# Half-height matmuls on pairs of tiles for the second dense product, and a new order of all steps

## The chip, the cores and the metric

The kernel runs on one core of a Trainium2 chip. The metric is the device time of one execution in microseconds (us). TensorE (PE) does the matmuls, VectorE (DVE) and ScalarE (ACT) read their results out of PSUM, GpSimd (POOL) helps with SBUF data, and SyncE (SP) issues nearly all transfers. Each engine works through its own instructions in the order in which they were written.

## The reference

`x` is 2048 tokens of 448 values. It is normalised once, and two branches of the result are added to it: an attention whose feature map is a pair of softmaxes (16 heads of 28), and a dense block with the mish activation.

```python
xn = _layernorm(x, axis=-1)
return x + _A_ref(xn, A_wqkv, A_w_phi, A_wo) + _B_ref(xn, B_w1, B_b1, B_w2)
# _A_ref:
pq = jnp.einsum("bhsd,hdf->bhsf", q, w_phi); pk = jnp.einsum("bhsd,hdf->bhsf", k, w_phi)
phi_q = jnp.concatenate([_softmax(pq), _softmax(-pq)], axis=-1)      # phi_k likewise
kv = jnp.einsum("bhsf,bhsd->bhfd", phi_k, v); z = jnp.einsum("bhsf->bhf", phi_k)
num = jnp.einsum("bhqf,bhfd->bhqd", phi_q, kv)
den = jnp.einsum("bhqf,bhf->bhq", phi_q, z)[..., None] + 1e-6
o = num / den                                                        # then o @ wo
# _B_ref:
h = jnp.einsum("bsd,df->bsf", x, w1) + b1                            # F = 1792
act = h * jnp.tanh(softplus(h)); jnp.einsum("bsf,fd->bsd", act, w2)
```

All operands are bf16.

## The kernel before

The 2048 tokens are 16 tiles of 128, taken as 8 pairs `u` (tiles `2u` and `2u+1`). A pair's normalised tokens lie transposed in `xnT`: 448 = 3 x 128 + 64 rows for each tile, arranged so that the halves of 64 rows of both tiles can be worked on side by side. Most products are therefore made of matmuls of 64 rows (half the height of the array), always one on the upper half for one tile and one on the lower half for the other. A step of this kind comes in three passes: A (upper half for the even tile, lower for the odd), B (the halves exchanged) and H (the odd quarter of 64 rows). The two halves of one pass write different PSUM banks; `pe_pass` makes a B pass wait until an A or H pass on the same banks has finished, and the other way round, on PE's own semaphore.

Every piece of work is a named step that records its instructions with what they read and write; waits follow from that. `ORDER` is a list of all step names, written out by hand or by a search, and it alone sets the order on every engine and the choice of PSUM banks (four pairs of banks; `take2` takes the free pair that was used longest ago, and a pair can be held over several steps). The steps:

- `z12` warm-up matmuls on `zeros` (L364), `b1` the bias, `wtk`/`wm` the weight products (L556, L580: `Wpq` and `Wpk`, projections with `w_phi` already in them), `xt` transposes of `xn`
- `v`, `k`, `q`: projections (L423, 64 x 448). ACT takes exponentials of `k` and `q` into `actT` rows and `Eq`; `kn` (DVE, POOL) normalises `k`; `kv` (L649, full 128 rows) sums the products of keys and values over all pairs in one bank, `kvz` adds the epsilon (DVE, L660) and issues the transpose into `KVZ` on SP; `e` transposes `Eq` into `EqT` on SP
- `f0.*`, `f1.*`: first dense product (L423, 64 x 512) for tiles 0 to 7 and 8 to 15, 14 chunks each, with mish on ACT (L699)
- `nd`: scores of one tile, 16 matmuls of 56 rows (L722), followed by six steps of DVE (L738 twice, L742, L744, L746, L748, L749), and `ot`, the transpose of a pair's result on SP
- `wo`: output product of a pair (L845, 64 x 448) in passes A, B, H; `g`: second dense product of one tile, 14 matmuls of 128 rows and 448 columns (L828). Both add into the same bank of the tile, held from the first to the last of the parts; then `finish` (DVE, L793) adds `x`, and `sto` stores. Tile 15 is cut: its last 64 columns come in a piece of their own (L807 to L810).
- `l2s`, `los`: the loads of `W2` and `Wo` on SP's queue

Of the kernel before, what the change touches and what calls it, by code (L numbers as in the profile page):

```python
# [38 lines left out]
class Program:  # L39
# [46 lines left out]
    def dma(self, eng, fn, r=(), w=(), tag=""):  # L86
        return self.op(eng, fn, r, w, dma=True, tag=tag)
# [61 lines left out]
wtk1b wmk0b lqT2 xt3a v2Ha wmk1a v2Ba lqT0 st1 v3Ha lqT1 lqT3 rs1a v3Aa v2Aa st4 rs4p pk v3Ba k3H lx0s k3A qd xn1d  # L149
wmq0d wmq1a k2H k3B lx6s pp k2A st5 q3A xn4d k2B q3B rs5p q2A xt1m l1ts q3H k1A q2H xn5p xt4m st0 v1Ad k1H st6 xt5m e7  # L150
rs0p q2B st7 xn0d v1Bd k1B v1Hd rs7p rs6p k4A k4H q1B k4B xn6d q1H q1A v4Ad k5H xn7d v4Hd k5A v4Bd v5Ad kn1.0 xt0m k5B
v5Bd k0B xt6m v5Hd xt7m v0Ba kn2.1 kn2.0 k0H k0A e3 k6H k6A kn0.0 e2 v6Ba l1ms k6B v0Ha kn0.1 v0Aa v6Aa v6Ha k7H k7A
q4B e6 k7B v7Aa v7Ha kn7.0 q4H q4A q6A q6H v7Ba e9 q6B kn6.0 f0.2B kn5.1 f0.0A f1.2A f0.2A f0.0H f1.2H kn6.1 e5 f1.3B
f0.2H f0.0B e12 f1.2B f1.3A kn4.1 f0.3B kn5.0 f1.3H e13 f0.3H f0.1B e4 f0.3A f0.1H f0.1A q7H q0A kn3.1 q0H kn4.0 q5B
e8 q0B q7B kv5 kn7.1 e0 kv0 kv2 q7A q5A f0.13A q5H f0.13B kv7 kv4 e10 kv6 f0.13H f0.6H f0.6A kn3.0 f0.10A f0.6B kn1.1
f0.10B kv3 kv1 ep f0.10H f1.7H f1.7A e11 f1.9A kvz f1.7B f0.12B f1.5B f0.12A f1.5H f0.5H f1.9H f0.12H l2s f1.9B f1.5A
f0.5A f1.1A nd3 f1.1B f0.5B e15 f1.0A f1.1H f1.13B f1.0H f1.13H f1.0B nd2 los f1.13A ot1m f1.8B f0.9H f1.8A f1.8H nd0
f0.11B f0.9A f0.11A f0.11H f0.7A f0.7H f0.8B nd6 e14 f0.8H f0.9B f0.7B e1 f0.8A f1.12H f1.12A f1.10A nd7 f1.10B f1.4H
f1.10H f1.12B ot3m f1.4A nd1 f1.6B f1.4B f0.4H f1.6A ot0m f0.4A wo1H f1.6H f0.4B nd4 wo1A wo3A wo1B wo3H nd5 ot2m g1
g3 g2 f1.11A f1.11H nd11 wo0B f1.11B wo3B wo0A nd13 wo0H nd10 g6 ot5m g0 g7 g11 nd12 wo2A wo5A sto1 ot6m wo5H wo2B  # L160
nd15 nd9 g10 sto0 g5 nd14 ot7m wo2H wo5B nd8 g4 g9 g14 g13 g12 g8 sto3 ot4m wo4H wo4A wo6B wo7B sto2 wo6H wo6A sto5
wo4B sto4 wo7H wob wo7A g15 stt14 sto6 stt15
"""


# [5 lines left out]
def _kernel(es, nc, A_x, A_wqkv, A_w_phi, A_wo, B_w1, B_b1, B_w2, out):  # L171
    def sb(name, shape, dtype):
        return es.enter_context(nc.sbuf_tensor(name, shape, dtype))
# [76 lines left out]
    def bank(b, n=1):  # L250
        return PS[:, b * TCW:(b + n) * TCW]
# [146 lines left out]
    def pe(fn, r, w, tag, after=()):  # L398
        return op("PE", fn, r=r, w=w, tag=tag, after=after)
# [201 lines left out]
    def xchunk(c, par):  # L601
        return c if c == 3 or par == 0 else 4 + c
# [187 lines left out]
    def finish(t):  # L790
        b = out_bank[t // 2] + t % 2
        n = width(t)
        op("DVE", lambda e: e.tensor_tensor(x_all[:, t, 0:n], bank(b)[:, 0:n], x_all[:, t, 0:n], ALU.add),  # L793
           r=[pb(b), ("x", t)], w=[("out", t)], tag=f"fin{t}")
        if t == LAST:
            last_columns(t, b ^ 1)
        if done[t] == done[t ^ 1] == parts_of(t):
            free2(out_bank[t // 2])
# [33 lines left out]
        if last:  # L832
            finish(t)

    def wo(u, part):
        places = [out_part(2 * u + par) for par in range(2)]
        todo = passes(part)

        def f(e):
            at = {par: [n for n, x in enumerate(todo) if x[1] == par] for par in range(2)}  # L840
            for n, (c, par, (lo, hi)) in enumerate(todo):
                b, first, last = places[par]
                cc = xchunk(c, par)
                w = width(2 * u + par)
                ins = e.matmul(bank(b)[:, 0:w], oT_of(u)[lo:hi, cc * P:(cc + 1) * P], Wo[lo:hi, cc, 0:w],  # L845
                               start=first and n == at[par][0], stop=last and n == at[par][-1])
# [132 lines left out]
```

## Time and profile before

| | |
|---|---|
| runs shown | 151.16, 151.43, 151.85 us, median 151.43 |
| the profiled execution | 150.73 us, span 148.7 us, granted clock 1.000 |
| PE busy | 144.0 us (97%), 1669 matmuls |
| DVE, ACT, POOL busy | 102.7, 74.7 and 38.9 us |
| 64 x 512 matmuls of the first dense product | 392, busy 44.8 us |
| 128-row matmuls of the second (L828) | 224, busy 42.9 us |

A matmul's end in the trace is modelled, and successive matmuls overlap, so busy times of groups on PE count some time twice where pieces alternate. What a piece of work on PE takes is read from one start to the next in the timeline. In a row of the timeline stand the start, the busy time, engine, line, operation, output and inputs, the shape, and how many instructions are merged.

### The profile page before, as it was taken

The numbers are of one execution on the slowest core, as the hardware profiler recorded it, in microseconds if no ns is written. First come the engines' busy times: TensorE is split into PE (matmuls) and PEld (weight loads), VectorE is DVE, ScalarE is ACT, GpSimd is POOL, SyncE is SP. The second block draws the span as 40 slices with busy tenths as digits, with TensorE's granted clock in tenths as the row PEclk, the third lists the DMA queues.
The fourth block names the chain that finished last, engine by engine and source line by source line (L and its number), as shares of the span: only waits on it lengthen the run. The fifth ranks groups of instructions, "written<-read, shape, count | busy, mean of one in ns | idle before, by whom it ended". The sixth has DMA issues, their size and how long they took to land.

```text
span 148.7 us, 3864 instructions
## 1 busy us (share of the span) xinstructions
PE 144.0 (97%) x1669; PEld 74.2 (50%) x1669; DVE 102.7 (69%) x229; ACT 74.7 (50%) x91; POOL 38.9 (26%) x53
## 2 busy tenths in 40 slices
PE   6899999999999999999999999999999999999992
PEld 2365555555444555444444445545555555555561
DVE  0699898996999930407787989529983999930072
ACT  4997999779999999567747661002000000000000
POOL 4424465179999992000000000000000000000000
PEclk9999999999999999999999999999999999999999
DMA  4997997799699069499956053210013130551005
GB/s 131 245 278 216 119 185 149 126 170 344 103 188 196 14 52 132 85 239 295 195 98 125 4 62 62 43 23 0 7 37 86 35 93 0 123 127 58 4 10 175
DMA packets 39964, 17.23 MB, mean 116 GB/s; under 512 B 33932, under 2 KB 39180, under 8 KB 39948
## 3 DMA queue, kind: packets, MB, share of 16 engines
q1 hardware_dynamic: 39776, 16.89, 54.4%
q8 instruction: 13, 0.21, 0.6%
q10 hardware_dynamic: 172, 0.10, 0.2%
q14 instruction: 3, 0.02, 0.0%
HBM read 7.02 MB, written 1.84 MB: 60 GB/s over the span
## 4 chain that ended last, share of the span: by engine, by line
PE 92%; DMA 3%; DVE 2%; SPq 1%; issue 0%
PE PS L423 50%; PE PS L828 29%; PE PS L845 7%; DMA Wkv<-in_A_wqkv_dram 3%; PE PS L722 3%; PE PS L649 2%; PE PS L580 1%; DVE xn L497 1%; SPq L270 1%; PE PS L556 0%; PE PS L505 0%; DVE x_all L793 0%; DVE Eq L512 0%; DVE x_all L814 0%
## 5 line engine op out<-in xcount | busy, mean ns | idle before, releaser
L423 PE MATMUL PS<-xnT,W 64*128 64x512 bf16 x392 | 44.8, 377 | 0.0
L828 PE MATMUL PS<-W,actT 128*128 128x448 bf16 (+1 forms) x224 | 42.9, 351 | 0.0
L699 ACT ACTIVATE actT<-PS,b1T 128x1024 bf16<-128x1024 f32 x28 | 29.8, 1112 | 22.1 <-PE PS L423 22.1
L828 PEld LDWEIGHTS PS<-W,actT 128*128 128x128 bf16 x224 | 21.5, 98 | 19.8 <-issue 0.3
L423 PEld LDWEIGHTS PS<-xnT,W 64*128 64x128 bf16 x392 | 17.9, 94 | 21.9 <-PE PS L423 1.9
L630 POOL TENSOR_TENSOR actT<-actT,rSk 128x896 bf16<-128x896 bf16 x16 | 26.6, 1699 | 5.1 <-DVE rSk L628 5.1
L793 DVE TENSOR_TENSOR x_all<-PS,x_all 128x448 bf16<-128x448 f32 (+1 forms) x16 | 9.2, 613 | 15.2 <-PE PS L845 10.5
L626 DVE TENSOR_REDUCE Sk<-actT 128x32 f32<-128x896 bf16 x16 | 16.6, 1037 | 1.1 <-ACT actT L618 1.1
L618 ACT ACTIVATE actT<-PS 128x896 bf16<-128x896 f32 x16 | 13.7, 920 | 1.8 <-PE PS L423 1.7
L423 PE MATMUL PS<-Wpk,xnT 64*128 64x448 bf16 x112 | 13.2, 349 | 0.0
L423 PE MATMUL PS<-Wkv,xnT 64*128 64x448 bf16 x112 | 12.9, 349 | 0.0
L423 PE MATMUL PS<-Wpq,xnT 64*128 64x448 bf16 x112 | 12.6, 349 | 0.0
L738 DVE COPY Sq<-PS 128x16 f32<-128x16 f32 x32 | 4.0, 167 | 12.0 <-PE PS L722 12.0
L462 DVE BATCH_NORM_STATS2 stats<-x_all 128x6 f32<-128x448 bf16 x14 | 8.4, 601 | 3.4 <-DMA x_all<-in_A_x_dram 3.4
L746 DVE TENSOR_TENSOR v_all<-v_all 128x464 f32<-128x464 f32 x16 | 10.3, 641 | 0.6
L742 DVE TENSOR_TENSOR v_all<-PS,Sq 128x464 f32<-128x464 f32 x16 | 10.3, 641 | 0.5
L749 DVE TENSOR_TENSOR xn<-v_all,rden 128x448 bf16<-128x448 f32 x16 | 10.0, 625 | 0.6
L744 DVE TENSOR_TENSOR v_all<-PS,Sq 128x464 f32<-128x464 f32 x16 | 10.1, 629 | 0.0
L680 ACT ACTIVATE actT<-PS 128x896 bf16<-128x896 f32 x10 | 8.6, 930 | 0.1
L423 PEld LDWEIGHTS PS<-Wpq,xnT 64*128 64x128 bf16 x112 | 5.4, 94 | 5.0 <-ACT actT L680 0.2
L423 PEld LDWEIGHTS PS<-Wkv,xnT 64*128 64x128 bf16 x112 | 5.4, 94 | 5.1 <-ACT actT L618 0.2
L423 PEld LDWEIGHTS PS<-Wpk,xnT 64*128 64x128 bf16 x112 | 5.3, 94 | 5.1 <-issue 0.2
(83 smaller groups left out, 118.8 us busy)
## 6 DMA issues: line engine op xcount, KB each, us to landing
W<-in_B_w_dram SPq DMA_DIRECT2D x1, 1568.0 KB, 7.9
out_dram<-x_all SPq DMA_DIRECT2D x7, 224.0 KB, 2.2
W<-in_B_w_dram SPq DMA_DIRECT2D x1, 1344.0 KB, 7.0
x_all<-in_A_x_dram SPq DMA_DIRECT2D x4, 224.0 KB, 3.1
x_all<-in_A_x_dram SPq DMA_DIRECT2D x2, 448.0 KB, 4.9
Wkv<-in_A_wqkv_dram SPq DMA_DIRECT2D x2, 336.0 KB, 4.8
Wo<-in_A_wo_dram SPq DMA_DIRECT2D x2, 336.0 KB, 6.3
W<-in_B_w_dram SPq DMA_DIRECT2D x2, 224.0 KB, 4.1
```

The source lines that it names most:

```text
L423: ins = e.matmul(o, lhs(c, k), rhs(c, k), start=first and n == at[par][0], stop=last and n == at[par][-1])
L618: op("ACT", lambda e, s=s: e.activation(E_of(u)[:, s, :, :], two(b, D), ACT.Exp, scale=1.0 if s == 0 else -1.0), r=[pb(b), pb(b + 1)], w=[ ...
L626: op("DVE", lambda e: e.tensor_reduce(Sk[u][:, s, :], Eh(), AX.X, ALU.add), r=[("E", u, s)], w=[("Sk", u, s)], tag=f"Sk{u}.{s}")
L630: op("POOL", lambda e: e.tensor_tensor(Eh(), Eh(), ap_on(rSk[u][:, s, 0:1], [[1, 2 * H], [0, DH]]), ALU.mult), r=[("E", u, s), ("rSk", u, ...
L699: op("ACT", lambda e: e.activation(actT[:, fc, q * 1024:(q + 1) * 1024], bank(b, 2), ACT.Mish, bias=b1T[:, fc:fc + 1]), r=[("b1T",), pb(b) ...
L742: op("DVE", lambda e: e.tensor_tensor(tv(t1[i]), num(0), sx(1), ALU.mult), r=[pb(b), pb(b + 1), ("Sq", i, 1)], w=[("t1", i)], tag=f"ta{t}")
L744: op("DVE", lambda e: e.tensor_tensor(tv(t2), num(1), sx(0), ALU.mult), r=[pb(b), pb(b + 1), ("Sq", i, 0)], w=[("t2",)], tag=f"tb{t}")
L746: op("DVE", lambda e: e.tensor_tensor(t1[i], t1[i], t2, ALU.add), r=[("t1", i), ("t2",)], w=[("t1", i)], tag=f"tc{t}")
L749: op("DVE", lambda e: e.tensor_tensor(o_sb[(t // 2) % 2][:, t % 2, :].rearrange("p (h d) -> p h d", d=DH), t1[i][:, :, 0:DH], ap_on(rden[i ...
L793: op("DVE", lambda e: e.tensor_tensor(x_all[:, t, 0:n], bank(b)[:, 0:n], x_all[:, t, 0:n], ALU.add), r=[pb(b), ("x", t)], w=[("out", t)], ...
L828: ins = e.matmul(bank(b)[:, 0:width(t)], actT[:, fc, tok(t)], W2[:, fc, 0:width(t)], start=first and fc == 0, stop=last and fc == FC - 1)
L845: ins = e.matmul(bank(b)[:, 0:w], oT_of(u)[lo:hi, cc * P:(cc + 1) * P], Wo[lo:hi, cc, 0:w], start=first and n == at[par][0], stop=last and ...
```

## The change

Steps `g0` to `g13` are gone. In their place, pairs 0 to 6 get two steps `G{u}A` and `G{u}B`. Each makes, for every one of the 14 chunks of 128 hidden values, one matmul with the upper 64 rows and one with the lower 64: in A the upper half works for the even tile and the lower for the odd, in B they are exchanged. `wo` and `G` share one function, `out_pair`, which gives each pass its place in the accumulation. Tiles 14 and 15 keep `g14` and `g15`. A step that loads `Wk` and `Wv` in one transfer (`lkvs`) is defined and not used by `ORDER`.

`ORDER` is new as a whole. Two lines of it, with the first steps and with the first of the new ones:

```diff
-pv table lx2s lba zero pm st2b lx3s lkms lps st3b lkts z12 pi b1 rs2p pw rs3a xn2d bd lx1s wtk0b lvms lx4s xn3d xt2b
...
+pw pi table lx2s lba zero st2b pm lx3s st3b lkms lps rs2p bd lkts z12 rs3a lx1s lvms xn2d b1 xn3d pv wtk0b xt2b pk
...
+G0A nd11 wo1A G1A nd12 G2A wo0A wo1H nd13 G1B wo1B G0B wo2H nd10 G2B wob ot5m wo2B wo0H wo3A wo0B nd14 G3A wo2A G3B
```

```diff
     def parts_of(t):
-        return 3 if f"wo{t // 2}F" in STEPS else 4
+        return (2 if f"wo{t // 2}F" in STEPS else 3) + (2 if f"G{t // 2}A" in STEPS else 1)
...
-    def wo(u, part):
+    def out_pair(u, part, todo, works, r, tag):
         places = [out_part(2 * u + par) for par in range(2)]
-        todo = passes(part)
 
         def f(e):
             at = {par: [n for n, x in enumerate(todo) if x[1] == par] for par in range(2)}
-            for n, (c, par, (lo, hi)) in enumerate(todo):
+            for n, (c, par, k) in enumerate(todo):
                 b, first, last = places[par]
-                cc = xchunk(c, par)
                 w = width(2 * u + par)
-                ins = e.matmul(bank(b)[:, 0:w], oT_of(u)[lo:hi, cc * P:(cc + 1) * P], Wo[lo:hi, cc, 0:w],
-                               start=first and n == at[par][0], stop=last and n == at[par][-1])
+                lhs, rhs = works(c, par, k, w)
+                ins = e.matmul(bank(b)[:, 0:w], lhs, rhs, start=first and n == at[par][0], stop=last and n == at[par][-1])
             return ins
-        pe_pass(f, [("oT", u)] + [("Wo", n) for n in range(4)], places[0][0], part, f"wo{u}{part}")
+        pe_pass(f, r, places[0][0], part, tag)
...
+    def ffn2_pair(u, part):
+        x = int(part == "B")
+
+        def works(fc, par, k, w):
+            return actT[k[0]:k[1], fc, tok(2 * u + par)], W2[k[0]:k[1], fc, 0:w]
+        out_pair(u, part, [(fc, r ^ x, HALF[r]) for fc in range(FC) for r in range(2)], works,
+                 [("W2",)] + [("act", fc, u // 4) for fc in range(FC)], f"G{u}{part}")
```

PE in the second dense product, before (L828 are the steps `g`, L722 `nd`, L845 `wo`, L423 the end of the first dense product):

```order
L722 MATMUL PS<-KVZ,EqT 128x60 x16
L845 MATMUL PS<-Wo,Wkv 128x448 x20
L722 MATMUL PS<-KVZ,EqT 128x60 x16
L828 MATMUL PS<-W,actT 128x448 x42
L423 MATMUL PS<-xnT,W 128x512 x8
L722 MATMUL PS<-KVZ,EqT 128x60 x16
L845 MATMUL PS<-Wo,Wkv 128x448 x6
L423 MATMUL PS<-xnT,W 128x512 x6
L845 MATMUL PS<-Wo,Wkv 128x448 x12
L722 MATMUL PS<-KVZ,EqT 128x60 x16
L845 MATMUL PS<-Wo,Wkv 128x448 x2
L722 MATMUL PS<-KVZ,EqT 128x60 x16
```

PE at the same place after (L848 is `out_pair`: with `W,actT` a half of `G`, with `Wo` a pass of `wo`; L726 is `nd`):

```order
L427 MATMUL PS<-xnT,W 128x512 x8
L848 MATMUL PS<-W,actT 128x448 x28
L726 MATMUL PS<-KVZ,EqT 128x60 x16
L848 MATMUL PS<-Wo,Wkv 128x448 x6
L848 MATMUL PS<-W,actT 128x448 x28
L726 MATMUL PS<-KVZ,EqT 128x60 x16
L848 MATMUL PS<-W,actT 128x448 x28
L848 MATMUL PS<-Wo,Wkv 128x448 x8
L726 MATMUL PS<-KVZ,EqT 128x60 x16
L848 MATMUL PS<-W,actT 128x448 x28
```

The full-height blocks are gone, a score product stands behind nearly every half of `G`, and three pairs of tiles are open at once; the first `G` comes when the first dense product is done.

PE from the warm-up to the first projections, before (L364 `z12`, L556 and L580 the weight products, L505 `xt`):

```order
L364 MATMUL PS<-zeros 128x512 x12
L693 MATMUL PS<-ident,b_rows 128x14
L556 MATMUL PS<-ident,Wkv 112x128 x8
L505 MATMUL PS<-ident,xn 128x128 x7
L556 MATMUL PS<-ident,Wkv 112x128 x8
L580 MATMUL PS<-Wbd,Eq 128x112 x8
L505 MATMUL PS<-ident,xn 128x128 x7
L423 MATMUL PS<-Wkv,xnT 128x448 x2
L580 MATMUL PS<-Wbd,Eq 128x112 x8
L423 MATMUL PS<-Wkv,xnT 128x448 x26
```

The same after:

```order
L368 MATMUL PS<-zeros 128x512 x12
L697 MATMUL PS<-ident,b_rows 128x14
L560 MATMUL PS<-ident,Wkv 112x128 x8
L509 MATMUL PS<-ident,xn 128x128 x7
L560 MATMUL PS<-ident,Wkv 112x128 x8
L509 MATMUL PS<-ident,xn 128x128 x7
L584 MATMUL PS<-Wbd,Eq 128x112 x16
L427 MATMUL PS<-Wkv,xnT 128x448 x22
```

The second transpose of `xn` went ahead of the weight product, which is now in one piece, and the two matmuls of `v` that stood within it went behind it.

POOL's first instructions of the kernel, before (`zeros` is what the warm-up multiplies):

```order
L339 MEMSET v_all 128x256
L316 MEMSET zeros 128x2
L327 MEMSET mask 112x4
L328 ISA
L328 AFFINE_SELECT mask<-mask 112x4
L331 AFFINE_SELECT mask<-mask 112x4
L319 MEMSET mhalf 128x2
```

and after:

```order
L340 MEMSET Wbd 112x512
L323 MEMSET mhalf 128x2
L324 MEMSET eps_col 128x1
L325 MEMSET ident 128x128
L326 ISA
L326 AFFINE_SELECT ident<-ident 128x128
L320 MEMSET zeros 128x2
```

`zeros` went from second to sixth place of the memory-setting and selecting instructions. Elsewhere: the eight `kv` steps stand on PE in two runs (192 and 64 matmuls) instead of three (96, 96, 64). On SP, `Wo`'s loads went ahead of most transposes of `Eq`, and `W2`'s load from behind the transpose of `KVZ` to behind the first two transposes `ot`. The numbers of instructions on DVE, ACT, POOL and of transfers are the same; PE has 196 matmuls more.

More of the change, by code (lines that the diff above doesn't have):

```diff
@@ L147 @@
 ORDER = """
-pv table lx2s lba zero pm st2b lx3s lkms lps st3b lkts z12 pi b1 rs2p pw rs3a xn2d bd lx1s wtk0b lvms lx4s xn3d xt2b
[L149 to L162, printed above, removed]
+pw pi table lx2s lba zero st2b pm lx3s st3b lkms lps rs2p bd lkts z12 rs3a lx1s lvms xn2d b1 xn3d pv wtk0b xt2b pk
@@ new lines @@
+f0.3A f0.1B f0.3B kn5.1 f0.2A f1.2H f0.2B f0.1H f0.2H f0.0B f1.3B f0.0H f0.0A f1.3A q5H e8 f1.3H q0B q5B q0A q5A q7B
+kn6.0 q0H e9 kn1.0 kn0.0 f0.7A e11 q7A q7H kv6 kv2 kv0 kn3.0 kv5 kv4 kv1 f0.6A f0.7H f0.6H f0.7B kn3.1 f0.12A kn7.0
+f0.12H f0.6B f0.12B kv3 kv7 f0.11A f1.9B e10 f0.11H f1.9H kvz f0.11B f1.5H f1.8B f1.5A f1.9A f1.8A f1.8H f1.13B e1 nd3
+f1.13H f1.5B e0 f1.13A f1.0B f1.10H nd2 f1.10A f1.0A f0.10H e15 f1.0H f0.10A f1.10B nd0 f1.1B f0.10B e14 f0.4H f1.1A
+f1.1H f0.4B nd1 f0.8A f0.4A f1.11H f1.11A ot1m f0.8B f1.4H ot0m f0.8H f1.4A nd6 f1.4B f1.11B f1.7B nd4 f1.7A f0.5A
@@ L163 @@
+f0.5H f1.7H f0.13B l2s f0.5B nd5 f1.6H f1.6A f0.13A f0.13H f0.9B f1.6B f0.9A f0.9H f1.12B nd7 ot2m ot3m f1.12H f1.12A
+G0A nd11 wo1A G1A nd12 G2A wo0A wo1H nd13 G1B wo1B G0B wo2H nd10 G2B wob ot5m wo2B wo0H wo3A wo0B nd14 G3A wo2A G3B
+ot6m nd15 G5B nd8 G5A wo5H nd9 G4B ot4m wo3H G6A wo5A ot7m G4A wo6A wo4B wo6H wo5B sto5 G6B wo4H sto2 wo3B wo7B wo4A
+wo6B wo7A wo7H sto0 sto3 g14 g15 sto6 sto1 sto4 stt14 stt15
 """
@@ L274, in load_main, with load_kv @@
             w=[(name, 0)], tag="ld" + name)
+    def load_kv(eng):
+        dma(eng, lambda e: e.dma_start(Wkv[:, 0:3, :], A_wqkv[0:384, D:3 * D].rearrange("(c p) f -> p c f", p=P)),
+            w=[("Wk", 0), ("Wv", 0)], tag="ldKV")
     def load_tail(eng, name, dst, src):
@@ L851, in wo, with works @@
                 finish(2 * u + par)
+    def wo(u, part):
+        def works(c, par, k, w):
+            cc = xchunk(c, par)
+            return oT_of(u)[k[0]:k[1], cc * P:(cc + 1) * P], Wo[k[0]:k[1], cc, 0:w]
+        out_pair(u, part, passes(part), works, [("oT", u)] + [("Wo", n) for n in range(4)], f"wo{u}{part}")
+    def ffn2_pair(u, part):
[4 more added lines that the diff above has]
+                 [("W2",)] + [("act", fc, u // 4) for fc in range(FC)], f"G{u}{part}")
     def store(a, b):
@@ L884, in _kernel @@
             add(f"wo{u}{part}", wo, u, part)
+        for part in "AB":
+            add(f"G{u}{part}", ffn2_pair, u, part)
         for s in range(2):
@@ L911, in _kernel @@
             add(f"l{n}m{c}", load_main, eng, "W" + n, t, A_wqkv[:, (i + 1) * D:(i + 2) * D])
+        add(f"lkv{c}", load_kv, eng)
         add(f"lkt{c}", load_tail, eng, "Wkv", Wkv, A_wqkv[:, D:3 * D])
```

5 lines of the change are left out of this document (added).

## The prediction

> **What bounds the kernel now.** I read the page first, then who waited for whom on PE, then PE's timeline where it changes from one kind of work to another.
>
> The page's head, its busy line, the granted clock and the chain that ended last:
>
> ```profile
> span 148.7 us, 3864 instructions
> ...
> PE 144.0 (97%) x1669; PEld 74.2 (50%) x1669; DVE 102.7 (69%) x229; ACT 74.7 (50%) x91; POOL 38.9 (26%) x53
> ...
> PEclk9999999999999999999999999999999999999999
> ...
> PE 92%; DMA 3%; DVE 2%; SPq 1%; issue 0%
> ```
>
> The waits of PE alone (us in total, times, longest):
>
> ```profile
> PE PS L364 <- POOL mask L327: 1.4, 1, 1.4
> PE PS L556 <- DMA Wkv<-in_A_wqkv_dram: 0.4, 1, 0.4
> ```
>
> PE is 97% busy, 92% of the chain is PE, and its only two idle times above the pipeline's own gaps lie before 6.72 us. So a reorder cannot gain by closing waits of PE, there are none left; it can lose by opening some. What can still be gained is time in which PE is "busy" but not at its pace. That shows in starts. Matmuls are pipelined, so the difference between the starts of two pieces is what a piece costs, not its busy time. PE in the order of time (start, busy, line, shape, count) around the second dense product (L828, 128 rows):
>
> ```profile
> 88.21 0.39 PE L722 MATMUL PS<-KVZ,EqT 56*128 56x60 bf16 x16
> 88.43 2.06 PE L845 MATMUL PS<-Wo,Wkv 64*128 64x448 bf16 x20
> 90.32 0.39 PE L722 MATMUL PS<-KVZ,EqT 56*128 56x60 bf16 x16
> 90.64 8.12 PE L828 MATMUL PS<-W,actT 128*128 128x448 bf16 x42
> ...
> 102.87 10.77 PE L828 MATMUL PS<-W,actT 128*128 128x448 bf16 x56
> 113.57 0.39 PE L722 MATMUL PS<-KVZ,EqT 56*128 56x60 bf16 x16
> ...
> 116.23 5.47 PE L828 MATMUL PS<-W,actT 128*128 128x448 bf16 x28
> 121.64 0.39 PE L722 MATMUL PS<-KVZ,EqT 56*128 56x60 bf16 x16
> ...
> 122.94 16.06 PE L828 MATMUL PS<-W,actT 128*128 128x448 bf16 x84
> 138.94 0.93 PE L845 MATMUL PS<-Wo,WqT 64*128 64x448 bf16 x8
> ```
>
> **Pace of the two forms.** 84 full-height matmuls take 138.94 - 122.94 = 16.00 us and 28 take 121.64 - 116.23 = 5.41; the 56 between them cost 10.59, so 0.1891 us each. Twenty half-height ones (L845) take 90.32 - 88.43 = 1.89, so 0.189 a pair: the two halves run beside each other. Fourteen tiles x 14 x 0.1891 = 37.07 us become 7 pairs of tiles x 28 pairs of halves x 0.189 = 37.04. The splitting by itself is worth nothing either way, though PE gets 196 matmuls more.
>
> [...]
>
> **Changes of form in the second dense product.** The score product (L722, 56 rows) is followed by half-height work after 88.43 - 88.21 = 0.22 us, but by L828 after 90.64 - 90.32 = 0.32: going in costs 0.10. Coming out: 10.70 - 56 x 0.1891 = 0.11, 5.41 - 28 x 0.1891 = 0.12, 16.00 - 84 x 0.1891 = 0.12. Before has four such blocks with an entry and an exit each and a fifth (tile 15) at the end. After, all score products, output products and halves of G are of the half-height kind and follow each other; only the entry before g14 is left, in place of the one before g15. Removed: 4 x (0.10 + 0.115) = 0.86 us, all of it on PE, which sets the end.
>
> **The k-v product** (L649, 128 rows) is also an island. Its rows:
>
> ```profile
> 50.82 0.95 PE L649 MATMUL PS<-actT,v_all 128*30 128x56 bf16 x96
> 51.70 1.31 PE L423 MATMUL PS<-Wpq,xnT 64*128 64x448 bf16 x12
> ...
> 58.48 0.71 PE L649 MATMUL PS<-actT,v_all 128*30 128x56 bf16 x64
> 59.11 7.97 PE L423 MATMUL PS<-xnT,W 64*128 64x512 bf16 x72
> 66.92 0.39 PE L722 MATMUL PS<-KVZ,EqT 56*128 56x60 bf16 x16
> ```
>
> 96 take 0.88, 64 take 0.63, so 32 take 0.25 and 0.13 is the exit; with an entry like the 0.10 above, an island costs 0.23. Before has three (96, 96, 64), after two (192, 64): 0.23 less.
>
> **The start.** PE from the warm-up on (L364 on zeros), and the four POOL instructions that say when `zeros` is there:
>
> ```profile
> 1.39 4.80 PE L364 MATMUL PS<-zeros 128*128 128x512 bf16 x12 [1.39 <-POOL mask L327]
> 6.12 0.18 PE L693 MATMUL PS<-ident,b_rows 14*128 14x14 bf16 x1
> 6.72 0.65 PE L556 MATMUL PS<-ident,Wkv 128*112 128x128 bf16 x8 [0.43 <-DMA Wkv<-in_A_wqkv_dram]
> ...
> 9.56 0.36 PE L423 MATMUL PS<-Wkv,xnT 64*128 64x448 bf16 x2
> 9.86 0.57 PE L580 MATMUL PS<-Wbd,Eq 112*128 112x112 bf16 x8
> 10.36 2.63 PE L423 MATMUL PS<-Wkv,xnT 64*128 64x448 bf16 x26
> ...
> 13.68 0.96 PE L580 MATMUL PS<-Wbd,WqT 112*128 112x112 bf16 x16
> 14.57 1.50 PE L423 MATMUL PS<-Wpk,xnT 64*128 64x448 bf16 x14
> ```
>
> ```profile
> 0.80 0.53 POOL L339 MEMSET v_all<- 128x256 uint32 x1 [0.29 <-POOLq L964]
> 1.18 0.15 POOL L316 MEMSET zeros<- 128x2 bf16 x1
> ...
> 1.82 0.10 POOL L319 MEMSET mhalf<- 128x2 f32 x1
> ...
> 2.36 0.29 POOL L322 TENSOR_SCALAR_AFFINE_SELECT ident<-ident 128x128 bf16<-128x128 bf16 x1
> ```
>
> Two things move here. First, the weight product L580 ran as 8, then 2 halves of L423, then 8; after, as one run of 16. The detour cost 9.86 - 9.56 = 0.30 for a pair worth 0.19, so 0.11, and the exit of L580: 16 take 14.57 - 13.68 = 0.89, 8 take 10.36 - 9.86 = 0.50, so 8 more cost 0.39 and the exit is 0.11. Removed: 0.22.
>
> Second, `zeros` is now written behind the 0.38 us of one large memset (1.18 - 0.80, as now) and also behind mhalf, eps and ident: from mhalf to the select 2.36 - 1.82 = 0.54, and up to 0.29 for the select. It starts by 0.80 + 0.38 + 0.54 + 0.29 = 2.01 at the latest, takes 0.15, and PE follows 0.06 later (1.39 against 1.33 now): the warm-up starts some 0.8 later, near 2.2. Nothing hides that: b1 comes near 6.9 instead of 6.12, and the first transpose, which now waits for its weights until 6.72, near 7.0. That is +0.28. It could be 0, if PE's inputs between 7 and 14 us, which do not move, then lie further ahead of PE. I take all of it, since its other side is open too: the twelve warm-up matmuls take 6.12 - 1.39 = 4.73 us, 0.39 each, where 512 columns take 0.217 later. The granted clock reads 9 throughout and does not show it, but at half pace (0.434) for nine or ten of them and full pace for the rest the sum is met: the array came to full pace some 4.1 us after the warm-up began. If that moment slips behind the first real work, work runs at half pace until it comes.
>
> **What moves without a price.** The k-norm, ACT and DVE steps change places with unchanged counts, under the cover of PE's 97%. W2's load goes behind the output transposes of pairs 1 and 0 on SP's queue, Wo's four loads come far earlier. The rows for that cover:
>
> ```profile
> W<-in_B_w_dram SPq DMA_DIRECT2D x1, 1568.0 KB, 7.9
> ...
> KVZ<-KVT SPq DMA_TRANSPOSE x1, 3.2
> ```
>
> ```profile
> L660 DVE TENSOR_SCALAR KVT<-PS,epsT 30x224 bf16<-30x224 f32 x4 | 1.8, 448 | 6.0 <-PE PS L649 6.0
> ```
>
> ```profile
> 61.13 1.23 SPq L666 DMA_TRANSPOSE KVZ<-KVT  x1
> ...
> 63.03 4.64 SPq L688 DMA_TRANSPOSE EqT<-actT  x1
> ```
>
> ```profile
> 71.49 0.26 DVE L738 COPY Sq<-PS 128x16 f32<-128x16 f32 x2 [1.05 <-PE PS L722]
> ...
> 74.51 0.25 DVE L738 COPY Sq<-PS 128x16 f32<-128x16 f32 x2
> ```
>
> DVE needs 3.02 us a tile (74.51 - 71.49), and the third of its six steps is the last that reads the banks. With three output pairs open, all score products of the dense stage share the fourth pair of banks. They stand at least one block of G apart, 28 x 0.0945 = 2.65 us, so the banks are free in time. Each half of G waits, on PE's own semaphore, for the other half of its pair of banks, with all of PE queued behind; the nearest such neighbours (wo1H to G1B, wo2H to G2B, G5B to G5A) have a score product between them, 0.22 us after a last matmul of 0.19: the wait is about over, a few hundredths at most.
>
> W2: it can be issued when pair 0's output transpose has been. From nd1 to G0A the order has 132 halves of 512 columns, 7.81 / 72 = 0.108 each (66.92 - 59.11), and three score products: 14.9 us. Needed: score 0.2, DVE 3.0 plus at most 1.0 of backlog from the three tiles ahead, 1.2 for one issue (61.13), the load 7.9: 13.3. Cover 1.6.
>
> KVZ: from the last k-v product to nd3, the first score product, stand 56 halves, 6.1 us. Needed: about 0.3 to the first of DVE's four steps, 1.8 for these, 3.2 for the transpose: 5.3. Cover 0.8, the smallest of all. Before, from 59.11 to 66.92, it was 2.5.
>
> **Sum.** -0.86 - 0.23 - 0.22 + 0.28 = -1.03 us. The profiled execution took 150.73 us for a span of 148.7; it would be 149.7. The median of the runs shown, 151.43, lies 0.7 above it, so the forecast is 151.43 - 1.03 = **150.4 us**.
>
> **Rivals.** *The array opens late* (0.20). If all twelve warm-up matmuls run at 0.434 us, they take 5.2 instead of 4.73 and real work begins near 7.5, 0.5 later than in the sum; if the pace changes only near 9, half of the 1.5 us until then is lost too. That takes back 0.5 to 1.25: 150.9 to 151.6, about no change. For it: 4.1 us out of 4.73 leaves little warm-up to spare. Against: nothing shows what sets the moment. [...]
>
> *Pairs do not keep their pace* (0.06). [...] L845 at 0.189 speaks against it, but reads Wo and the attention output, not W2 and actT. [...]
>
> *KVZ comes late at nd3* (0.10), the case on the slow side. Its transpose stands on SP's queue behind two of EqT, and the 63.03 row shows an issue on that queue held 4.64 us, 3.4 more than one takes. If KVZ's were held so, PE would stand 3.4 - 0.8 = 2.6 at nd3: 150.4 + 2.6 = 153.0. It decides from 0.8 us late on, and the kernel is slower than before from 1.8. Against: that issue stood right behind the 7.9 us load of W2, which now comes after.
>
> *The changes of form are not gone* (0.04): if the array has to be emptied between 56-row and 64-row work of other operands too, nothing is won: 151.7 with the late start. The 0.22 of L722 into L845 speaks against.
>
> **Chances.** A measurement of this kernel tells 0.5% (0.76 us) from no change. Forecast 0.60; the rivals above 0.40. Faster by more than that: 0.62, the forecast and a mild form of the late array. Same: 0.27. Slower: 0.11, KVZ and the worst of the rest. The forecast's own range is 150.1 to 150.8: the start's 0.28 not paid on one side, the 0.4 by which the runs of before lie off their median on the other. For 8 in 10 the range takes that 0.4 below 150.1 too, and the late array above: 149.7 to 151.6.
>
> **What would show it.** Right: L848's halves of W2 and actT at 0.189 us a pair; every score product followed after 0.22; one change of form after 90 us; L653 in two pieces; PE waiting nowhere after 8 us. Wrong: PE waits for W2, for KVZ, or for DVE at a score product; a pair above 0.192; first transpose after 7.4 us.

## The result: 151.78 us, slower by 0.4% instead of faster by 0.7%

Before took 151.2 us (median of 22 runs), after 151.78 (22 runs, 151.45 to 153.67): a ratio of 1.0040 with an interval of 1.0023 to 1.0057, so 0.35 to 0.86 us slower. The forecast was 150.4 with a range of 149.7 to 151.6. The two profiled executions lie further apart than the medians (152.43 us for a span of 149.9 against 150.73 for 148.7): before's was a quick one, 0.5 below its median, after's 0.65 above its own.

The profile after: the page's head, busy line, clock and chain, and below them the waits of PE alone (us in total, times, longest).

```profile
span 149.9 us, 4249 instructions
...
PE 143.7 (96%) x1865; PEld 75.5 (50%) x1865; DVE 102.5 (68%) x229; ACT 74.8 (50%) x91; POOL 38.9 (26%) x53
...
PEclk9999999999999999999999999999999999999999
...
PE 91%; ACT 3%; DVE 2%; POOL 1%; issue 1%; POOLq 0%
```

```profile
PE PS L368 <- POOL mask L331: 2.3, 1, 2.3
PE PS L509 <- DVE xn L501: 1.2, 1, 1.2
PE PS L427 <- ACT actT L703: 0.2, 1, 0.2
```

Two waits are new: 1.2 us for VectorE's normalising step (L501), and one for ScalarE's mish (L703). ScalarE, which had no share of the chain before, has 3%. The first wait in the order of time: PE (L368 is the warm-up, L560 and L584 the weight products, L509 the transposes of `xn`, the second row of them those of pair 3, called the third pair's in what follows, L427 the first long run of `v`), then VectorE, then POOL.

```profile
2.29 5.27 PE L368 MATMUL PS<-zeros 128*128 128x512 bf16 x12 [2.29 <-POOL mask L331]
7.50 0.18 PE L697 MATMUL PS<-ident,b_rows 14*128 14x14 bf16 x1
7.60 0.65 PE L560 MATMUL PS<-ident,Wkv 128*112 128x128 bf16 x8
...
10.28 0.56 PE L509 MATMUL PS<-ident,xn 128*128 128x128 bf16 x7 [1.19 <-DVE xn L501]
10.69 1.16 PE L584 MATMUL PS<-Wbd,Eq 112*128 112x112 bf16 x16
11.78 2.25 PE L427 MATMUL PS<-Wkv,xnT 64*128 64x448 bf16 x22
```

```profile
6.29 0.89 DVE L501 TENSOR_SCALAR xn<-x_all,mv,rstd 128x448 bf16<-128x448 bf16 x3 [1.26 <-POOL rstd L477]
7.71 0.17 DVE L516 CAST b1T<-PS 128x14 f32<-128x14 bf16 x1 [0.53 <-PE PS L697]
7.80 2.43 DVE L501 TENSOR_SCALAR xn<-x_all,mv,rstd 128x448 bf16<-128x448 bf16 x3
```

```profile
7.13 1.08 POOL L543 TENSOR_TENSOR Wbd<-Wraw,mask 112x224 bf16<-112x224 bf16 x2 [0.88 <-DMA Wraw<-in_A_w_phi_dram]
8.14 0.54 POOL L343 MEMSET v_all<- 128x256 uint32 x1
8.53 0.58 POOL L352 MEMSET KVT<- 128x512 uint32 x1
9.04 0.57 POOL L348 MEMSET actT<- 128x256 bf16 x2
```

The same three instructions of VectorE take 0.89 us at 6.29 and 2.43 at 7.80, and the second group is done at 10.23, soon after POOL's last fill (9.61). All of the delay lies in the first of the three:

```profile
7.80 1.93 DVE L501 TENSOR_SCALAR xn<-x_all,mv,rstd 128x448 bf16<-128x448 bf16 x1
```

The first one at 6.29 takes 0.40. This one ends at 9.73, 0.13 us after the last of the four fills. In the kernel before the first of these fills ran at 0.80 us; now all stand behind `Wbd`. PE comes to the long run of `v` and `k` at 11.78 instead of 10.36.

The second new wait: SP's queue, ScalarE and PE (L273 is W1's main load, L692 the transposes of `Eq`, L684 the exponential of `q`).

```profile
33.32 0.59 SPq L273 DMA_DIRECT2D W<-in_B_w_dram  x1
33.96 1.24 SPq L692 DMA_TRANSPOSE EqT<-actT  x1
```

```profile
42.76 1.73 ACT L684 ACTIVATE actT<-PS 128x896 bf16<-128x896 f32 x2 [1.06 <-PE PS L427]
44.50 1.28 ACT L703 ACT_TABLE_LOAD   x1
45.80 3.12 ACT L703 ACTIVATE actT<-PS,b1T 128x1024 bf16<-128x1024 f32 x3
```

```profile
47.97 2.33 PE L427 MATMUL PS<-xnT,W 64*128 64x512 bf16 x20 [0.18 <-ACT actT L703]
```

Tile 2's transpose now stands behind W1's load (in the kernel before it was tile 6's) and lands at 42.69, where the load lands at 40.28; the exponential that reuses its buffer starts at 42.76, 1.06 us after ScalarE is free (the row names PE, whose operands had long been there), and mish begins at 45.80.

The dense stage itself, halves of G (W, actT) and score products (L726):

```profile
116.53 2.81 PE L848 MATMUL PS<-W,actT 64*128 64x448 bf16 x28
119.18 0.38 PE L726 MATMUL PS<-KVZ,EqT 56*128 56x60 bf16 x16
119.40 2.81 PE L848 MATMUL PS<-W,actT 64*128 64x448 bf16 x28
```

Fourteen pairs take 119.18 - 116.53 = 2.65 us, 0.189 each, and a score product costs 119.40 - 119.18 = 0.22 with half-height work behind it. That is what the prediction said, and after 90 us the only change of form left is the one ahead of `g14`, at 141.82. The k-v products (L653):

```profile
55.07 2.07 PE L653 MATMUL PS<-actT,v_all 128*30 128x56 bf16 x192
57.06 4.08 PE L427 MATMUL PS<-xnT,W 64*128 64x512 bf16 x36
```

192 take 57.06 - 55.07 = 1.99 us where 6 x 0.25 + 0.13 = 1.63 was expected; matmul by matmul, the extra lies in two gaps of 0.13 and 0.19 us without any wait behind them.

### The profile page after: what moved, and what is told of

Same layout as the page of the kernel before. It is cut to its first block, busy times and chain, and to the rows that moved or that the text cites. A ratio compares the mean times of both kernels' runs of the same rounds, so it can differ in the third digit from the quotient of the medians.

```text
span 149.9 us, 4249 instructions
## 1 busy us (share of the span) xinstructions
PE 143.7 (96%) x1865; PEld 75.5 (50%) x1865; DVE 102.5 (68%) x229; ACT 74.8 (50%) x91; POOL 38.9 (26%) x53
## 4 chain that ended last, share of the span: by engine, by line
PE 91%; ACT 3%; DVE 2%; POOL 1%; issue 1%; POOLq 0%
PE PS L427 46%; PE PS L848 32%; PE PS L368 4%; PE PS L832 3%; PE PS L726 2%; PE PS L653 2%; DVE xn L501 2%; ACT actT L703 1%; PE PS L584 1%; ACT actT L684 1%; ACT L703 1%; PE PS L509 0%; DVE x_all L797 0%; POOL Wbd L340 0%; POOL ident L326 0%
## 5 line engine op out<-in xcount | busy, mean ns | idle before, releaser
L427 PE MATMUL PS<-xnT,W 64*128 64x512 bf16 x392 | 45.0, 377 | 0.2 <-ACT actT L703 0.2
L848 PE MATMUL PS<-W,actT 64*128 64x448 bf16 x392 | 39.4, 349 | 0.0
L703 ACT ACTIVATE actT<-PS,b1T 128x1024 bf16<-128x1024 f32 x28 | 30.0, 1114 | 10.3 <-PE PS L427 10.3
L427 PEld LDWEIGHTS PS<-xnT,W 64*128 64x128 bf16 x392 | 18.2, 94 | 21.6 <-PE PS L427 1.7
L848 PEld LDWEIGHTS PS<-W,actT 64*128 64x128 bf16 x392 | 18.5, 94 | 16.8
L427 PE MATMUL PS<-Wpk,xnT 64*128 64x448 bf16 x112 | 13.7, 349 | 0.0
L427 PE MATMUL PS<-Wkv,xnT 64*128 64x448 bf16 x112 | 13.2, 349 | 0.0
L427 PE MATMUL PS<-Wpq,xnT 64*128 64x448 bf16 x112 | 13.1, 349 | 0.0
L684 ACT ACTIVATE actT<-PS 128x896 bf16<-128x896 f32 x10 | 8.7, 932 | 1.2 <-PE PS L427 1.2
L501 DVE TENSOR_SCALAR xn<-x_all,mv,rstd 128x448 bf16<-128x448 bf16 (+2 forms) x21 | 7.7, 426 | 1.7 <-POOL rstd L477 1.7
L427 PEld LDWEIGHTS PS<-Wpq,xnT 64*128 64x128 bf16 x112 | 5.7, 94 | 5.0
L427 PEld LDWEIGHTS PS<-Wpk,xnT 64*128 64x128 bf16 x112 | 5.6, 94 | 4.9 <-issue 0.3
```

Of the source, the lines that this page charges most:

```text
L427: ins = e.matmul(o, lhs(c, k), rhs(c, k), start=first and n == at[par][0], stop=last and n == at[par][-1])
L501: op("DVE", lambda e, t=t, lo=lo, hi=hi, at=at: e.tensor_scalar(X[:, at:at + hi - lo], x_all[:, t, lo:hi], mv[:, t, 0:1], rstd[:, t:t + 1] ...
L684: op("ACT", lambda e, s=s: e.activation(Eq_of(u)[:, :, s, :].rearrange("p i (h n) -> p i h n", n=64)[:, :, :, 0:QP], two(b, D).rearrange(" ...
L703: op("ACT", lambda e: e.activation(actT[:, fc, q * 1024:(q + 1) * 1024], bank(b, 2), ACT.Mish, bias=b1T[:, fc:fc + 1]), r=[("b1T",), pb(b) ...
L848: ins = e.matmul(bank(b)[:, 0:w], lhs, rhs, start=first and n == at[par][0], stop=last and n == at[par][-1])
```

## The experiments

Theory 1: POOL's late fills hold VectorE's normalising step. Theory 2: the late warm-up sets the start. Theory 3: tile 2's transpose behind W1's load delays ScalarE and with it PE. Rival to all: the pairs never brought what was forecast. Ratios are to the kernel before, run on the same chip. From chip to chip its median lies between 151.04 and 151.40 us, so kernels that ran on different chips are compared better by their ratios than by their times.

**Fills early (theory 1).** `pp` is cut in two, since its third buffer is still in use.

```diff
-st2b pm lx3s
+st2b pm pv pk pp12 lx3s
...
-xn3d pv wtk0b xt2b pk wtk1b
+xn3d wtk0b xt2b wtk1b
...
-k3A pp qd
+k3A pp0 qd
```

> The changed kernel with POOL's constant fills of v_all, KVT and the first two actT buffers put directly behind the mask, where POOL is idle until 5.2 us; nothing else differs. Theory 1 (these fills, beside VectorE's normalising step of tile 6, hold it back): the step that took from 7.80 to 9.73 us ends by about 8.6, the third pair's transposes (10.28) start by about 9.1, and the kernel is 1.0 to 1.2 us faster than the changed kernel, 150.6 to 150.8 us, about 0.997 of the kernel before. Theory 2 (the late warm-up alone sets the start): the transposes move by 0.2 us at the most and the time stays near 151.7.

Measured: 150.38 us, ratio 0.9945 (0.9925 to 0.9965), 1.40 below the changed kernel. VectorE's row and the third pair's transposes:

```profile
7.84 0.90 DVE L501 TENSOR_SCALAR xn<-x_all,mv,rstd 128x448 bf16<-128x448 bf16 x3
```

```profile
9.22 0.55 PE L509 MATMUL PS<-ident,xn 128*128 128x128 bf16 x7
```

0.90 instead of 2.43 at the same place, the third pair's transposes at 9.22 instead of 10.28, with the warm-up as late as ever (2.29) and b1 at 7.52. PE's only wait left in this profile is the warm-up's; the wait for mish is gone too, though SP's order was not touched. Theory 1 holds, and it gave more than the 1.0 to 1.2 expected.

**The kernel before with late fills (theory 1, from the other side).**

```diff
-pv table lx2s
+table lx2s
...
-xn2d bd lx1s
+xn2d bd pv pk pp12 lx1s
...
-rs4p pk v3Ba
+rs4p v3Ba
...
-lx6s pp k2A
+lx6s pp0 k2A
```

> The kernel before with one thing alone: the same constant fills (v_all, KVT, two actT buffers) on POOL directly behind the two products of Wbd, as the changed kernel has them. Theory 1: VectorE's normalise of tile 6, which starts near 7.75, ends only with the fills, near 9.9; the third pair's transposes go from 9.06 to about 10.2, and the kernel is 0.9 to 1.5 us slower, 152.0 to 152.6 us, ratio 1.006 to 1.010. If the fills do not matter to VectorE: within 0.2 us of 151.1.

Measured: 152.29 us, ratio 1.0102 (1.0065 to 1.0139). One VectorE row and one PE row:

```profile
7.72 2.65 DVE L497 TENSOR_SCALAR xn<-x_all,mv,rstd 128x448 bf16<-128x448 bf16 x3
```

```profile
10.42 0.57 PE L505 MATMUL PS<-ident,xn 128*128 128x128 bf16 x7 [1.40 <-DVE xn L497]
```

Four constant fills in another place make the old kernel about 1.2 us slower (1.0 to 2.1 by the ratio), with a wait of 1.40 us where the changed kernel has 1.19. Again the first of the three instructions ends 0.13 us after POOL's last fill (9.88 after 9.75). Taking a fill from ahead of `zeros` also moves the warm-up, from 1.39 to 0.95, but the first weight product still waits for its load (6.68 against 6.72), so the start is otherwise as it was.

**Zeros first (theory 2).** One word of the order moves; the fills stay late.

```diff
-pw pi table lx2s lba zero st2b pm
+zero pw pi table lx2s lba st2b pm
```

> The changed kernel with the zeros of the warm-up written first on POOL, so that the warm-up starts near 0.9 us instead of 2.29; the fills stay where they were. Theory 2 (the late warm-up is what the start lost): b1's product comes down from 7.50 to about 6.1, the first transposes from 7.60 to about 6.7, and 0.8 to 1.2 us of the time go, to about 150.8. Theory 1 (POOL's fills hold VectorE's normalise until they end near 9.6): the first transposes come earlier, but the third pair's stay near 10.2, and the time falls by 0.2 us at the most.

Measured: 153.39 us, ratio 1.0155 (1.0122 to 1.0188), 1.6 slower than the changed kernel, which neither theory had. The warm-up began at 0.95 and the third pair's transposes came at 10.53 (theory 1's half is right), but then the clock fell. Stretches of the span, with PE's busy time (after the length) and the granted clock (PEclk, the third figure from the end), first this kernel, then the changed one:

```profile
6.38:9.79 3.41, 1.70 (x23) 1.38 (x23) 3.27 (x5) 2.58 (x7) 2.48 (x7) 1.00 1.13 297
9.79:16.62 6.83, 6.09 (x45) 3.67 (x47) 6.03 (x19) 2.65 (x5) 1.31 (x4) 0.50 0.76 170
```

```profile
7.40:10.81 3.41, 2.22 (x35) 1.97 (x35) 3.10 (x7) 1.46 (x3) 2.21 (x6) 1.00 1.18 295
```

The warm-up took 5.24 us (0.95 to 6.19), 0.44 a matmul, where 512 columns take 0.217 later. Of the 3.41 us from the end of b1's product (6.38) to the fall of the clock (9.79) at a clock of 1.00, PE was busy for 1.70, and then it worked at 0.50 until 16.62 us. In the changed kernel PE waits nearly as long for VectorE (1.19 instead of 1.40) but is busy for 2.22 us of a stretch as long at the same steps (7.40 to 10.81), and the clock stays at 1.00. The mean granted clock was 0.977 to 0.989 in all six executions of this kernel, and 0.998 or more in 21 of the 22 of the changed one.

**Fills early and zeros first.** Both edits above together.

> The changed kernel with POOL's fills of v_all, KVT and two actT buffers early (as in e1_pool_early) and the zeros of the warm-up first on POOL. Theory 2 in its new form (the late warm-up costs time once the fills are out of the way): b1's product at about 6.2 instead of 7.5, first transposes near 6.8, v of the third pair 0.5 to 0.8 us earlier than 10.67, time 149.6 to 149.9. Rival (an early warm-up is followed by idle stretches of TensorE, and the granted clock falls as it did in e2_zero_first, 0.5 in the slice from 11.4 us): the time rises above 151. Rival 2 (the transposes wait for Wkv's landing and VectorE's normalise anyway): within 0.2 us of 150.4.

Measured: 150.07 us, ratio 0.9937 (0.9923 to 0.9950). The clock stays at 1.0, and the long run of `v` starts at 10.09 instead of 10.67 with the fills alone. Of that 0.6 us, 0.1 to 0.3 arrives in the time (0.9945 to 0.9937 in ratios, 150.38 to 150.07 in medians); the intervals of the two ratios overlap, so that this is not clear of noise. This kernel is faster than both given ones.

**SP's order around W1 (theory 3).**

```diff
-v5Ad e3 k5B v5Bd kn2.1 k7B v7Ba e6 k7A
+v5Ad e6 k5B v5Bd kn2.1 k7B v7Ba l1ms k7A
...
-q6H l1ms v0Ba
+q6H e3 v0Ba
```

> The changed kernel with three DMA issues on SP's queue exchanged: the transposing load of Eq for tile 6, then W1's main load, then the one for tile 3, then tile 2 (before this: 3, 6, W1, 2), so that W1's load starts earlier and the transpose of tile 2 no longer lands at 42.7. Theory 3 (that transpose behind W1's load delays ScalarE and with it the dense stage): ScalarE's first mish comes about 0.9 us earlier than 45.80, the two stalls of 0.20 and 0.36 us in front of the first half-rows of columns 0 and 3 go, and the time falls by 0.4 to 0.6 us to about 151.3. Rival (those stalls are absorbed later, or the load's own landing moves them): within 0.2 us of 151.8.

Measured: 151.73 us, ratio 1.0037 (1.0023 to 1.0051): no change. SP's issue of the transposes of tiles 3 and 2, which now both stand behind the load:

```profile
32.33 6.33 SPq L692 DMA_TRANSPOSE EqT<-actT  x2
```

It took 6.33 us, tile 2's transpose landed at 42.16, and the exponential started at 42.23 instead of 42.76. The experiment did not remove what it was to remove. It did shorten PE's waits for mish, from 0.55 us by starts to 0.20, and the time did not follow beyond the noise (151.78 to 151.73).

**W1's load on ScalarE's queue (theory 3).**

```diff
-k5B v5Bd
+k5B l1ma v5Bd
...
-q6H l1ms v0Ba
+q6H v0Ba
```

> The changed kernel with W1's main load issued from ScalarE's queue, in an idle stretch of ScalarE near 31.4 us, instead of from SP's queue at 33.3 us ahead of tile 2's transpose of Eq. The fills stay late. Theory 3 (the transpose behind that load costs the dense stage its two stalls): tile 2's transpose lands before 39 instead of at 42.69, ScalarE's next exponential starts near 41.7 instead of 42.76, the first mish near 44.8 instead of 45.80, the stalls of 0.20 and 0.36 us go, and the kernel takes 151.2 to 151.4 us. Rival (the two transfers share the DMA engines, and what the one gains the others lose): stalls come at the transposes of pairs 0, 6 or 7 or at W1's first use instead, and the time stays at 151.7 or above.

Measured: 153.79 us, ratio 1.0154 (1.0109 to 1.0200). ScalarE issued the load at 29.60, earlier than meant. Its issue, its landing (6.4 us later), and PE:

```profile
29.60 0.45 ACTq L273 DMA_DIRECT2D W<-in_B_w_dram  x1
```

```profile
W<-in_B_w_dram ACTq DMA_DIRECT2D x1, 1344.0 KB, 6.4
```

```profile
35.56 0.74 PE L427 MATMUL PS<-Wpq,xnT 64*128 64x448 bf16 x6 [2.60 <-DMA xnT<-xn]
```

The rival, and more of it: pair 6's transpose, issued on SP at 29.11, landed at 35.43, about when W1 did (29.60 + 6.4), though another queue carried W1. The profiled execution is 2.2 us above the kernel's median, so the row gives the place and not the amount. Theory 3's mechanism is there in the trace, a transpose beside a load in flight landed about when the load did (35.43 against 36.0 here) or after it (42.69 against 40.28 in the changed kernel); its price in the changed kernel was not separated.

**The kernel before with pairs alone.** `g1` becomes `G0A`, `g0` becomes `G0B`, and so on in the places of before; `g14` moves next to `g15`.

```diff
-nd5 ot2m g1 g3 g2 f1.11A f1.11H nd11
+nd5 ot2m G0A G1A G1B f1.11A f1.11H nd11
```

> The kernel before, in its own order of steps, with one thing alone: the second dense product of tiles 0 to 13 as pairs of halves (the first tile of each pair's place taken by the first half, the second tile's by the second half; tile 14 put directly ahead of tile 15). The prediction's term for this alone is a gain of 0.86 us: 150.3 us, ratio 0.9943. If the half-height pairs or the changes of form bring nothing, the ratio is 0.999 to 1.001; if the pairs lose pace, above 1.002.

Measured: 151.54 us, ratio 1.0027 (1.0012 to 1.0043): slower. PE at the first three halves:

```profile
90.86 8.35 PE L848 MATMUL PS<-W,actT 64*128 64x448 bf16 x84
99.04 1.03 PE L427 MATMUL PS<-xnT,W 64*128 64x512 bf16 x8
100.46 0.39 PE L726 MATMUL PS<-KVZ,EqT 56*128 56x60 bf16 x16 [0.39 <-DVE x_all L797]
```

The 84 halves take 8.18 us where 3 x 2.65 = 7.95 is their pace: `G1B` directly behind `G1A` waits 0.23 for it, and so do `G6B` behind `G6A` and `wo4H` behind `G4B` (three times 0.231). And `nd11` waits for a bank that both tiles of pair 1 leave late, 0.555 us more than its place takes. 3 x 0.231 + 0.555 = 1.25 eats the 0.86.

**The same with those neighbours parted.**

```diff
-nd5 ot2m G0A G1A G1B f1.11A f1.11H nd11 wo0B f1.11B
+nd5 ot2m G1A G0A G1B f1.11A f1.11H wo0B nd11 f1.11B
...
-G4A G6A G6B G4B sto3
+G4A G6A G4B G6B sto3
```

> The kernel before with the second dense product of tiles 0 to 13 as pairs, as in e4_before_G, but with no two halves of one pair back to back (there each of three such places cost 0.231 us) and with one Wo product put ahead of nd11 (there nd11 waited 0.555 us for tile 3's addition). If those four stalls are what ate the prediction's 0.86 us: 150.2 to 150.4 us, ratio 0.9935 to 0.9955. If the term of 0.86 us itself is wrong: 151 us or more.

Measured: 150.56 us, ratio 0.9957 (0.9942 to 0.9972), that is 0.42 to 0.88 us faster than before, and 1.0 faster than with the neighbours together. The four stalls are gone; 0.86 lies at the edge of the interval.

**Single tiles among the halves.** The kernel with early fills, each half exchanged for a whole tile.

```diff
-G0A nd11 wo1A G1A nd12 G2A wo0A
+g0 nd11 wo1A g2 nd12 g4 wo0A
```

> The kernel of e1_pool_early with each half of a pair replaced in its place by one whole tile of the pair (the same count of matmuls' columns, full height), so that 14 full-height blocks stand singly among half-height ones. By the prediction's price of a change of form (0.10 us in, 0.115 us out): 14 x 0.215 = 3.0 us slower than e1_pool_early, 153.4 us. If the change of form costs nothing: 150.4; if the pairs lose pace and the changes cost 0.1 in all: about 151.8.

Measured: 153.40 us, ratio 1.0152 (1.0130 to 1.0173), 3.02 above the kernel with early fills (3.1 by the ratios). Score product, whole tile (L832), score product, whole tile:

```profile
118.61 0.39 PE L726 MATMUL PS<-KVZ,EqT 56*128 56x60 bf16 x16
118.93 2.82 PE L832 MATMUL PS<-W,actT 128*128 128x448 bf16 x14
121.69 0.40 PE L726 MATMUL PS<-KVZ,EqT 56*128 56x60 bf16 x16
122.01 2.82 PE L832 MATMUL PS<-W,actT 128*128 128x448 bf16 x14
```

In: 118.93 - 118.61 = 0.32 instead of 0.22. Out: 121.69 - 118.93 = 2.76 against 2.65. The price of a change of form, 0.215 for both ways, is shown by 14 of them (14 x 0.215 = 3.01).

**The k-v products in other runs.** Three kernels on the one with both edits; first 5 + 3 pairs. There `kv1` comes after a chunk of the first dense product has overwritten its keys, so that its sums are not the right ones; work and shapes are the same.

```diff
-kv5 kv4 kv1 f0.6A
+kv5 kv4 f0.6A
...
-kv3 kv7 f0.11A
+kv3 kv7 kv1 f0.11A
```

> The kernel of e5_early_zero with the k-v product of the second pair (kv1) moved from the first run of k-v products to the second, so that they are 5 + 3 pairs (160 + 96 matmuls) instead of 6 + 2 (192 + 64). In the longer run of e5_early_zero there are two gaps with no wait behind them, 0.13 us near the 90th matmul and 0.19 us some 64 matmuls later. If a gap comes at a count of matmuls since the run began, the first stays, the second goes: 0.15 to 0.2 us faster than 150.07, about 149.9. If the gaps belong to a place in the program and not to the run's length: both stay, 150.1.

Measured: 150.18 us, ratio 0.9948 (0.9923 to 0.9973). Both gaps stayed in the run of 160 (0.133 near its 90th matmul, 0.196 at its end), none in the run of 96.

```diff
-kv6 kv2 kv0 kn3.0 kv5 kv4 kv1 f0.6A f0.7H f0.6H
+kv6 kv2 kv0 f0.6A f0.7H kn3.0 kv5 kv4 kv1 f0.6H
```

> The kernel of e5_early_zero with the k-v products in three runs of 3, 3 and 2 pairs (96, 96, 64 matmuls), two half-height blocks put between the first two. By the count of matmuls both gaps go (0.32 us) and one more change of form in and out comes (0.21 us): 0.1 us faster than 150.07, about 150.0; in the trace the three runs have no gap over 0.05 us inside. If the gaps belong to the place: 0.2 us slower, 150.3.

Measured: 150.87 us, ratio 0.9985 (0.9964 to 1.0006). The first run of 96 has one gap of 0.13, the others none. `f0.6A` was brought ahead of ScalarE's exponential and waited for it: it starts 0.63 us after the last k-v product, where 0.13 is usual, so 0.50 is a new wait in place of the old gaps.

```diff
-q7A q7H kv6 kv2 kv0 kn3.0 kv5
+q7A kv6 kv2 kv0 q7H kn3.0 kv5
```

> The kernel of e5_early_zero with the k-v products in three runs of 3, 3 and 2 pairs again, with the one short half-height block q7H between the first two, so that the first block behind them comes no earlier for ScalarE than in e5_early_zero (in e10_kv332 it waited 0.63 us for ScalarE). If the two gaps come from the length of the run: they go (0.32 us), one change of form in and out comes (0.21 us): 0.1 us faster than 150.07. If a gap can come in a run of 96 too, as one of 0.13 us did in e10_kv332: 150.1 to 150.2.

Measured: 150.17 us, ratio 0.9922 (0.9900 to 0.9943), level with the kernel it is built on (0.9937). The timeline of PE:

```profile
52.64 0.95 PE L653 MATMUL PS<-actT,v_all 128*30 128x56 bf16 x96
53.53 0.37 PE L427 MATMUL PS<-Wpq,xnT 64*128 64x448 bf16 x2
53.82 0.95 PE L653 MATMUL PS<-actT,v_all 128*30 128x56 bf16 x96
54.70 4.08 PE L427 MATMUL PS<-xnT,W 64*128 64x512 bf16 x36
```

Runs of 96 at 0.88 to 0.89 have no gap inside; what they save, the third island costs. Long runs have gaps, but the one in a run of 96 above says that length alone is not the rule; the cause stays open.

## Why the prediction was wrong

**Pace of the pairs: right** (0.189, over fourteen pairs that follow each other). **Changes of form: right**: 14 of them cost 3.02 us where the prediction's price makes 3.01; what the array does in that time was not shown. The pairs alone bring 0.42 to 0.88 us, provided that no half follows its partner directly. The prediction had such neighbours down for a few hundredths with a score product between them, and in the changed kernel there is no stall; without one they cost 0.23.

**The k-v product: mis-sized.** The term was -0.23 for one island fewer, but the run of 192 brings 0.32 of gaps, so +0.09 stands in its place. Three islands without the gaps measured the same as two with them (0.9922 and 0.9937, with intervals that overlap).

**The weight product: mis-sized.** From 10.69 to 11.78 the run of 16 takes 1.09 us, against 0.89 for the 16 of `Wpq`. The detour's 0.22 went, and a wait of 0.20 for the evacuation of the second eight, which `v` had hidden, came: -0.02 in place of -0.22.

**The late zeros: not contradicted in size, not right in form.** +0.28 was forecast; with the fills out of the way an earlier warm-up brings 0.1 to 0.3, within the noise. In the profiled execution the twelve took 5.21 us (2.29 to 7.50), 0.434 each and so at half the later pace (0.217) throughout, as the rival of the late array had it, and the first transpose came at 7.60, beyond the 7.4 named as a sign of error. But that length belongs to a run, not to the change: from the start of the warm-up to b1 it is 5.21 us here, 4.73 in the profile of before, 4.29 in the profile with SP's exchanged order (2.29 to 6.58, the same first steps), 4.18 to 5.24 over all. What sets it was not shown.

**W2 and KVZ: right.** PE waits for neither.

**The step that failed is "What moves without a price".** It let steps change places under the cover of PE's 97% busy time, without asking what they would run beside, and "The start" took PE's inputs between 7 and 14 us as things "which do not move". POOL's fills were counted there only for what they put ahead of `zeros`; that `pv`, `pk` and `pp` go behind `Wbd` has no term at all. But 97% is a mean over the span. In the kernel before, this step of VectorE was already the last thing ahead of the third pair's transposes:

```profile
7.75 1.25 DVE L497 TENSOR_SCALAR xn<-x_all,mv,rstd 128x448 bf16<-128x448 bf16 x3
```

```profile
9.06 0.56 PE L505 MATMUL PS<-ident,xn 128*128 128x128 bf16 x7
```

It ended at 9.00. Moving `pv`, `pk` and `pp` behind `Wbd` put 1.5 us of POOL beside a step on which PE waits next, and the step took 2.43 us instead of 1.25: it ended at 10.23. The price is 1.40 us in the changed kernel (fills early against late) and about 1.2 in the kernel before (fills late against early). The rows: 2.43 and 2.65 us beside the fills, 0.89 and 0.90 without them, 1.25 beside `Wbd` alone. VectorE's first instruction did not end soon after the POOL instruction under way at its start (`Wbd`, until 8.21 in the changed kernel), but only after POOL's whole unbroken series, both in the changed kernel (9.73, the series 9.61) and in the kernel before with late fills (9.88 and 9.75). In the profile with SP's exchanged order it ended before the last fill did (9.64, last fill ending at 9.88). What holds it back, no row names. The risk could have been seen before the run: the step's 1.25 beside `Wbd` against 0.90 at 6.42 and the fills' rows stood in the profile of before, and the order said where the fills go.

**The sum.** With early fills the change measures 150.38 against 151.12, so -0.74 (by the ratio -0.53 to -1.13). The forecast of -1.03 lies in that interval, but that is partly luck: the terms as re-sized give -0.86 + 0.09 - 0.02 + 0.28 = -0.51, just outside it, and 0.2 is not accounted for. The price of late fills as measured in the kernel before, about 1.2, makes +0.5 of the -0.74; measured is +0.58 (0.35 to 0.86), so the two experiments agree. The waits for mish in the profile after (0.55 us by starts) are inside the 1.40: with early fills they are gone from that profile. As 0.30 of them is back in the profile with 5 + 3 pairs, they are partly a matter of the run. The forecast's 150.4 was also counted from 151.43, the median of the three runs shown, 0.2 above the median of 22.

## What to carry to other kernels

When an order is new as a whole, check every moved step of VectorE and GpSimd for what runs beside it on the other, not only for its own duration: constant fills belong where VectorE has no step like this tensor_scalar on the critical path (2.43 and 2.65 us beside the fills here, 0.90 without), here POOL's idle stretch from 2.8 to 5.2 us. A mean of 97% busy says nothing of the slack at one place. Price a change of array form by the starts around it (0.215 us a round trip here), and keep work that accumulates into the same banks apart (0.231 us at each of three places where it followed directly).

## What was not expected of the hardware

- An earlier warm-up alone made the kernel 1.6 us slower: the granted clock was 0.50 from 9.79 to 16.62 us, after a stretch at 1.00 (6.38 to 9.79) in which PE was busy for 1.70 us. The clock fell with three waits (0.73, 0.33 and 1.40 us, the fall inside the last) and little work between them. Only one profile shows the place, but all six executions have a lower mean clock and take 153.07 us or more. What lowers the clock was not measured.
- Runs of 160 and 192 short k-v matmuls have gaps of 0.13 and 0.19 us about 64 matmuls apart (the second in two parts in some profiles), with no semaphore behind them.
- A transpose of SBUF data in flight beside a load of 1344 KB landed about when that load did or after it, on the load's queue (tile 2 after 8.7 us, 33.96 to 42.69, the load at 40.28) or on another (pair 6 after 6.3 us, against 3.1 in the changed kernel).
